# Top-32 attention into a capacity-dropping MoE: all products by the sign on GpSimd, the pick's table in PSUM, one order for all steps

## The chip, the cores and the metric

The kernel runs on one core of one Trainium2 chip. The metric is the device time of one execution in microseconds (us). The kernel before takes 996.0 us, the median of three runs (993.81, 996.0 and 996.81). The profiled execution took 994.79 us, with a span of 993.1 us from its first to its last instruction and a mean granted TensorE clock of 0.987.

## What is computed

The first part is attention over 8 batches and 8 heads, with 576 rows of 64 numbers per head. Of each row of scores only the 32 largest stay. The output, as 4608 tokens of 512 numbers, goes into a mixture of eight experts, each of which keeps at most 80 tokens.

```python
scores = scale * np.matmul(q, k.transpose(0, 1, 3, 2))          # (8, 8, 576, 576)
kth = np.partition(scores, -32, axis=-1)[..., -32:-31]
scores = np.where(scores >= kth, scores, -1e9)
attn = softmax(scores)                                          # exp, sum, divide
x = np.matmul(attn, v) -> (4608, 512)
expert_idx = argmax(x @ w_gate); gate_w = softmax(...)[expert_idx]
for e in range(8):
    tok = the (at most 80) tokens of expert e with the largest gate_w
    out[tok] = gate_w[tok] * (relu(x[tok] @ w1[e]) @ w2[e])
```

## The kernel before

**Tiling.** A pair of heads of one batch is one `n`; there are 32 of them. A *unit* is up to 128 score rows of one head, a tile of 128x576. A pair has nine units: four row blocks for each of the two heads (taken two by two, as `t` = 0 to 3 with `h` = 0 and 1), and one for the 64 rows left over of both heads together (`t` = 4, `h` = 2). That makes 288 units.

**What one unit goes through.** `front` (L216) multiplies the scores of one `t`, both heads at once, into four PSUM banks that `four` (L194) hands out, and ScalarE copies them to SBUF (L233, "the evacuation"). VectorE takes the eight largest of each of six groups of 96 (L241, letter G below), and then in three rounds the 24 largest of those 48 candidates (L252 and L260). With the 24th as a bar, ScalarE computes the sign of bar minus score, with its sum as a count (L257). The product of score and sign (L264, called `y`) turns what lies above the bar negative, so that a further maximum over 576 numbers (L266) finds the next eight. The *pick* (L269) compares the count with a table `past` of nine numbers and so chooses the threshold, the 32nd largest, out of nine candidates. `below` (L273) makes a mask from it: on GpSimd for even units (L280), on ScalarE for odd ones (L278). `turn_w` (L300) transposes scores and mask on TensorE, and ScalarE applies the exponential (L323 and L325). `back` (L328) multiplies by V, `over` (L340) takes the reciprocal of the sums on VectorE, and `divide` (L350) scales on ScalarE (L359).

**The order.** `run` (L428) writes the order out by hand (`manual_schedule`). A step `i` works on several units at once: G on unit `i`, the pieces b to e of the search on unit `i-1`, the product `y` on `i-2`, the maximum g on `i-3`, and the pick h and the mask m on `i-4`. A string of letters gives the order inside the step; odd and even steps have different strings (L459). The product is on GpSimd for odd units and on VectorE for even ones. After the letters a step emits, where they are due, `turn_w` of unit `i-4`, `divide`, `front` of unit `i+4`, and `back`. Every engine works through its own instructions in the order in which they are written, and waits by semaphores. So on ScalarE the work of a step is: the mask (odd units), the sign of unit `i-1`, the two exponentials, the two scalings, and last the evacuation of the scores of unit `i+4`. Of nine steps, five have a `front`. In three of the other four the same four banks serve another purpose: to transpose the next pair's Q and K (`turn`, copied at L214), to transpose the output (`norm`, copied at L376), and for the gate's logits (copied at L388).

**The scores' banks.** `four` takes a new tile from a pool of one buffer for each use. A use may begin when the readers of the use before are done.

**The weights.** The weights of experts 0 to 3 (4 MB for each) are loaded during the attention, in `slow`. Those of expert 4 are loaded when the attention's SBUF is free (`finish`, L733), and those of experts 5 to 7 when an earlier expert is done with its buffer.

Of the kernel before, what the change touches and what calls it, by code (L numbers as in the profile page):

```python
# [27 lines left out]
def kernel(  # L28
# [120 lines left out]
    class Attention:  # L149


        def __init__(self, stack, lean):
            self.lean = lean
            pool = lambda name, bufs, **kw: stack.enter_context(tc.tile_pool(name=name, bufs=bufs, **kw))
            self.nat, self.qkp, self.rows = pool("nat", 1), pool("qkp", 2), pool("rows", 2)
            self.small, vpool = pool("small", 4), pool("vpool", 1)
            self.ps_s, self.ps_w, self.ps_c = (pool(n, k, space=PSUM) for n, k in (("ps_s", 1), ("ps_w", 1), ("ps_c", 2)))
            self.qk, self.turned, self.lg = {}, {}, {}
            self.s, self.top, self.cnt, self.y, self.mask, self.w, self.xn = ({} for _ in range(7))
            self.thr, self.z = thr_all, z_all  # L160
            self.odd = set()


            self.vb = []
            for j in range(1 if lean else 3):
                t = vpool.tile([P, NK, 2, D + 1], F32, name=f"vb{j}")
                nc.gpsimd.memset(t[:, :, :, D : D + 1], 1.0)
                nc.gpsimd.memset(t[: P - TL, NF, :, :], 0.0)
                self.vb.append(t)

            self.xT = vpool.tile([P, NK * P], F32, name="xT")
            nc.gpsimd.memset(self.xT[:, S:], 0.0)
# [18 lines left out]
                t[P - TL :, NF, :, :D], v[one, 2 * hp : 2 * hp + 2, NF * P :, :].rearrange("o h p d -> p (o h) d"))  # L191
            self.qk[n] = tiles

        def four(self):  # L194
            return self.ps_s.tile([P, 4, 512], F32, name="sp", tag="sp")

        def turn_in(self, ps, t, cs=range(NK)):

# [3 lines left out]

        def turn(self, n):

            four = self.four()
            ps = [four[:, 2 * j : 2 * j + 2, :].rearrange("p j c -> p (j c)") for j in range(2)]
            both = self.qkp.tile([P, 2, S], F32, name="both", tag="both")
            self.turned[n] = both[:, 0, :], both[:, 1, :]
            for j, src in enumerate(self.qk.pop(n)):
                self.turn_in(ps[j], src.rearrange("p c h d -> p c (h d)"))  # L210
                if n == 0:
                    nc.scalar.copy(both[:, j, :], ps[j][:, :S])
            if n > 0:
                nc.scalar.copy(both, four.rearrange("p (k j) c -> p k (j c)", k=2)[:, :, :S])  # L214

        def front(self, n, t):  # L216

            qT, kT = self.turned[n]
            m = P if t < NF else TL
            i = n * UPP + 2 * t  # L220
            ps = self.four()
            for j in range(2):
                for h in range(2):
                    d = slice(D * h, D * h + D)
                    o = ps[:, 2 * h + j, :HS] if t < NF else ps[TL * h : TL * h + TL, j, :HS]
                    nc.tensor.matmul(o, lhsT=qT[d, t * P : t * P + m], rhs=kT[d, j * HS : (j + 1) * HS], start=True, stop=True)  # L226
            g = 2 if t < NF else 1
            s = self.rows.tile([P, 2 * S], F32, name="s", tag="s", bufs=2 if self.lean else 5)
            for h in range(g):
                self.s[i + h] = s[:, h * S : (h + 1) * S]  # L230
            for j in range(0, 2 * g, 2 if i == 0 else 2 * g):
                w = 2 if i == 0 else 2 * g
                nc.scalar.activation(s[:, j * HS : (j + w) * HS].rearrange("p (j c) -> p j c", c=HS), ps[:, j : j + w, :HS],  # L233
                                     Act.Copy, scale=TINY)

        def parts(self, i):
# [8 lines left out]
        def search(self, i):  # L245

            s, cand = self.s[i], self.top[i]
            top = self.top[i] = self.small.tile([P, G0 // 8 - 1, 8], F32, name="top", tag="top")
            w9 = self.small.tile([P, 16], F32, name="w9", tag="w9")
            for r in range(G0 // 8):  # L250
                dst = top[:, r, :] if r < G0 // 8 - 1 else w9[:, :8]
                nc.vector.max(out=dst, in_=cand)  # L252
                if r == G0 // 8 - 1:

                    sign = self.rows.tile([P, S], BF16, name="sign", tag="sign")
                    cnt = self.small.tile([P, 1], F32, name="cnt", tag="cnt")
                    nc.scalar.activation(sign, s, Act.Sign, bias=w9[:, 7:8], scale=-1.0, accum_out=cnt)  # L257
                yield
                if r < G0 // 8 - 1:
                    nc.vector.match_replace(out=cand, in_to_replace=dst, in_values=cand, imm_value=LOW)  # L260
                    yield
            y = self.rows.tile([P, S], F32, name="y", tag="y", bufs=1)
            engine = nc.gpsimd if i in self.odd else nc.vector
            engine.tensor_tensor(out=y, in0=s, in1=sign, op=Alu.mult)  # L264
            yield
            nc.vector.max(out=w9[:, 8:], in_=y)  # L266
            yield
            pick = self.small.tile([P, TOP_K - G0 + 1], F32, name="pick", tag="pick")
            nc.vector.scalar_tensor_tensor(out=pick, in0=past, scalar=cnt, in1=w9[:, 7:], accum_out=self.thr[:, i : i + 1],  # L269
                                           op0=Alu.is_equal, op1=Alu.mult)  # L270
            yield

# [9 lines left out]
        def search_all(self, i):  # L282

            s = self.s[i]
            top = self.top[i] = self.small.tile([P, TOP_K // 8, 8], F32, name="top", tag="top")
            scr = self.rows.tile([P, S], F32, name="y", tag="y", bufs=1)
            nc.vector.max(out=top[:, 0, :], in_=s)
            for r in range(1, TOP_K // 8):
                nc.vector.match_replace(out=scr, in_to_replace=top[:, r - 1, :], in_values=s if r == 1 else scr,
                                        imm_value=LOW)  # L290
                nc.vector.max(out=top[:, r, :], in_=scr)
            nc.vector.tensor_copy(self.thr[:, i : i + 1], top[:, TOP_K // 8 - 1, 7:8])
# [7 lines left out]
        def turn_w(self, n, t):  # L300
# [2 lines left out]
            g = 2 if t < NF else 1  # L303
            if i == NU - 1 and not self.lean:

                ab = self.four().rearrange("p h (c r) -> p h c r", r=P)
            else:
                ab = self.ps_w.tile([P, 2, NF, P], F32, name="ab", tag="ab")
            cc = self.ps_c.tile([P, 512], F32, name="cc", tag="cc")
# [51 lines left out]
        def norm(self, n, b, hp, bi, nb, cs=range(NK)):  # L361
# [7 lines left out]
            if NF in cs:  # L369
                nc.sync.dma_start(xv[one, NF * P :, cols].rearrange("o p d -> p o d"), xn[:TL, NF:, :])  # L370
            yield 1
            ps = self.four()[:, :2, :].rearrange("p j c -> p (j c)")
            at = slice(cs[0] * P, min(S, cs[-1] * P + P))
            self.turn_in(ps, xn, cs)
            xT = self.xT
            nc.scalar.copy(xT[:, at], ps[:, at])  # L376
            yield 1
            lp = self.four()[:, 0, : NK * E].rearrange("p (c e) -> p c e", e=E)
            for c in cs:
                for r in range(0, P, TL):  # L380
                    nc.tensor.matmul(lp[r : r + TL, c, :], lhsT=xT[:, c * P + r : c * P + r + TL], rhs=wg[:, hp, :],
# [46 lines left out]
        def run(self, slow):  # L428
# [17 lines left out]
            def step(i, last):  # L446
# [8 lines left out]
                    first[i] = self.parts(i)  # L455

                back = dict(a=0, b=1, c=1, d=1, e=1, y=2, g=3, h=4, m=4)

                for c in "ghmGbGycGdGGGeaz" if i % 2 else "GbGhmgcGdGeGGyaz":  # L459
                    if c == "G":  # L460
                        if 0 <= i < NU:
                            next(first[i])
                    elif c == "a":
                        if 0 <= i < NU:
                            next(first[i], None)
                            second[i] = self.search(i)
                            next(second[i])
                    elif c == "z":
                        for u in drawn:
                            self.over(*u)  # L470
                    elif c == "m":
                        if 0 <= i - back[c] < NU:
                            self.below(i - back[c])
                    elif i - back[c] in second:
                        next(second[i - back[c]])
# [257 lines left out]
    def finish(wpool, full):  # L733

        stack = ctx.enter_context(ExitStack())
        late = stack.enter_context(tc.tile_pool(name="late", bufs=1))
        for dma in load_w(4, late):
            dma()
        sl = stack.enter_context(tc.tile_pool(name="sl", bufs=1))
        fs = stack.enter_context(tc.tile_pool(name="fs", bufs=2))  # L740
        ps_x = stack.enter_context(tc.tile_pool(name="ps_x", bufs=2, space=PSUM))
# [119 lines left out]

    slow = clear()
    with ExitStack() as main:
        wpool = main.enter_context(tc.tile_pool(name="wpool", bufs=4))
        for e in range(4):
            slow += load_w(e, wpool, 4)
        with ExitStack() as stack:
            att = Attention(stack, False)
            att.run(slow)
        finish(wpool, False)  # L870
    with tc.If(nc.values_load(bad[0:1, 0:1]) > 0):
# [4 lines left out]
            with tc.For_i(0, B) as b:  # L876
                att.batch(b)
        with ExitStack() as again:
            wpool = again.enter_context(tc.tile_pool(name="wpool2", bufs=4))
            for e in range(4):  # L880
                for dma in load_w(e, wpool):
                    dma()
            finish(wpool, True)
# [31 lines left out]
```

## Time and profile before

| what | number |
|---|---|
| time, median of three | 996.0 us |
| span of the profiled execution | 993.1 us |
| attention: from the start to about 869 us; routing and experts after it | |
| VectorE busy | 870.6 us (88%) |
| TensorE busy / its weight loads | 885.5 us (89%) / 704.9 us (71%) |
| ScalarE busy | 797.2 us (80%) |
| GpSimd busy | 451.9 us (46%) |
| product `y` on VectorE / on GpSimd | 144 of 747 ns / 144 of 1283 ns |
| mask on GpSimd / on ScalarE | 144 of 1723 ns / 144 of 780 ns |
| pick on VectorE | 288 of 241 ns in the mean |
| evacuation of the scores on ScalarE | 161, 1040 ns in the mean |

The shares of busy time are means over the whole span, in which the attention takes seven eighths. An instruction's duration reaches from its start to its end; where an engine overlaps the start of one with the end of the one before, the distance from start to start is shorter, and the durations add up to more than the busy time.

### The profile page before, as it was taken

Reading aid. Unit: us, or ns where it says so; the run is one execution under the profiler, and the core shown is the slowest. Engines: PE = TensorE matmul, PEld = TensorE weight load, DVE = VectorE, ACT = ScalarE, POOL = GpSimd, SP = SyncE. Lnnn points to the kernel's source line nnn. Section 1 sums busy time; section 2 is a strip of 40 time slices with the busy share of each in tenths; the row PEclk is TensorE's granted clock in tenths of the full one; section 3 lists DMA queues with packets and bytes.
Section 4 is the critical chain, followed back from the end, with each engine's and each line's share of the span. In section 5 each row is a group of like instructions: output and inputs, shape, how many; then the busy total and the mean of one; then the engine's idle time right before and its main releaser. Section 6 shows DMA issues by size and latency. Waiting matters only on the chain.

```text
span 993.1 us, 35590 instructions
## 1 busy us (share of the span) xinstructions
PE 885.5 (89%) x13368; PEld 704.9 (71%) x13368; DVE 870.6 (88%) x5072; ACT 797.2 (80%) x1652; POOL 451.9 (46%) x330
## 2 busy tenths in 40 slices
PE   5899999998989989899899999999899898679996
PEld 3677777776767777677677777777677676668896
DVE  5899999999999999999999999999999999571110
ACT  3899999999999989999999999999899999601110
POOL 2445555555455545554555555555455555302111
PEclk9999999999999999999999999999999999979998
DMA  3344453333332323333333322222222100044920
GB/s 72 97 126 131 129 134 92 92 92 92 91 79 62 87 82 86 92 92 93 88 82 83 91 49 51 50 50 50 50 50 49 41 23 14 16 170 142 382 76 28
DMA packets 167893, 85.76 MB, mean 86 GB/s; under 512 B 117792, under 2 KB 154656, under 8 KB 167712
## 3 DMA queue, kind: packets, MB, share of 16 engines
q1 hardware_dynamic: 166688, 80.78, 29.7%
q0 software_dynamic: 1024, 2.62, 0.9%
q8 instruction: 107, 1.75, 0.7%
q14 instruction: 74, 0.61, 0.2%
HBM read 63.19 MB, written 20.19 MB: 84 GB/s over the span
## 4 chain that ended last, share of the span: by engine, by line
DVE 53%; PE 24%; ACT 18%; issue 5%; DMA 1%; POOL 0%; POOLq 0%; SPq 0%; ACTq 0%; DVEq 0%
DVE cand L241 17%; DVE w L266 12%; DVE cand L260 6%; DVE y L264 6%; ACT s L233 4%; DVE top L252 4%; PE yp L799 4%; ACT wT L325 3%; PE sp L201 3%; PE cc L336 3%; ACT sign L257 3%; DVE pick L269 3%; ACT mask L278 2%; PE sp L226 2%; PE ab L316 2%
## 5 line engine op out<-in xcount | busy, mean ns | idle before, releaser
L241 DVE MAX8 cand<-s 128x8 f32<-128x96 f32 x1728 | 393.9, 250 | 8.9 <-ACT s L233 8.8
L280 POOL TENSOR_SCALAR mask<-s,thr_all 128x576 bf16<-128x576 f32 x144 | 248.2, 1723 | 144.9 <-DVE pick L269 121.8
L264 POOL TENSOR_TENSOR y<-s,sign 128x576 f32<-128x576 f32 x144 | 184.8, 1283 | 277.3 <-DVE pick L269 128.0
L336 PEld LDWEIGHTS cc<-vb,wT 128*64 128x64 f32 x5760 | 181.7, 138 | 111.2 <-ACT wT L325 98.5
L257 ACT ACTIVATE sign<-s,w 128x576 bf16<-128x576 f32 x288 | 225.4, 783 | 22.8 <-DVE w L252 22.2
L336 PE MATMUL cc<-vb,wT 128*64 128x65 f32 x5760 | 204.0, 225 | 40.6 <-ACT wT L325 38.9
L266 DVE MAX8 w<-y 128x8 f32<-128x576 f32 x288 | 217.8, 756 | 2.5 <-POOL y L264 2.5
L226 PE MATMUL sp<-both 64*128 64x288 f32 (+1 forms) x1280 | 202.1, 435 | 15.0 <-ACT part L388 6.5
L233 ACT ACTIVATE s<-sp 128x1152 f32<-128x1152 f32 (+1 forms) x161 | 167.3, 1040 | 12.7 <-PE sp L226 11.9
L316 PE MATMUL ab<-ident,s 128*128 128x128 f32 x1148 | 175.6, 282 | 0.0
L325 ACT ACTIVATE wT<-ab 128x1024 f32<-128x1024 f32 (+1 forms) x159 | 148.8, 936 | 0.0
L226 PEld LDWEIGHTS sp<-both 64*128 64x128 f32 (+1 forms) x1280 | 105.6, 179 | 53.8 <-ACT part L388 8.5
L316 PEld LDWEIGHTS ab<-ident,s 128*128 128x128 f32 x1148 | 127.5, 141 | 11.6 <-issue 0.9
L321 PEld LDWEIGHTS <-mask 128*128 128x128 bf16 x1440 | 92.1, 98 | 42.4 <-ACT mask L278 19.6
L252 DVE MAX8 top<-cand 128x8 f32<-128x48 f32 x576 | 116.9, 203 | 0.0
L260 DVE MATCH_REPLACE8 cand<-top,cand 128x48 f32<-128x48 f32 x576 | 112.9, 196 | 0.0
L278 ACT ACTIVATE mask<-s,thr_all 128x576 bf16<-128x576 f32 x144 | 112.3, 780 | 0.4
L264 DVE TENSOR_TENSOR y<-s,sign 128x576 f32<-128x576 f32 x144 | 107.6, 747 | 4.5 <-ACT sign L257 4.5
L359 ACT ACTIVATE xn<-cc,z_all 128x64 f32<-128x64 f32 (+1 forms) x320 | 86.5, 318 | 1.4 <-DVE z_all L348 0.8
L316 PE MATMUL cc<-ident,s 128*128 128x128 f32 x288 | 78.9, 274 | 0.3 <-ACT xn L359 0.2
L269 DVE SCALAR_TENSOR_TENSOR pick<-past,cnt,w 128x9 f32<-128x9 f32 x288 | 69.5, 241 | 0.2 <-DVE z_all L348 0.2
L323 ACT ACTIVATE wT<-cc 128x256 f32<-128x256 f32 (+1 forms) x160 | 56.2, 351 | 12.0 <-PE cc L321 11.3
(188 smaller groups left out, 965.7 us busy)
## 6 DMA issues: line engine op xcount, KB each, us to landing
w<-in_moe_w_dram SPq DMA_DIRECT2D x32, 512.0 KB, 4.7
w<-in_moe_w_dram SPq DMA_DIRECT2D x8, 2048.0 KB, 9.8
out_dram<-zero SPq DMA_DIRECT2D x9, 1024.0 KB, 6.3
qn<-in_q_dram SPq DMA_DIRECT2D x64, 128.0 KB, 2.6
kn<-in_k_dram SPq DMA_DIRECT2D x64, 128.0 KB, 2.5
vb<-in_v_dram SPq DMA_DIRECT2D x64, 128.0 KB, 2.6
xd<-xn SPq DMA_DIRECT2D x32, 256.0 KB, 4.3
qn<-in_q_dram SPq DMA_DIRECT2D x32, 32.0 KB, 2.5
```

The source lines that it names most:

```text
L226: nc.tensor.matmul(o, lhsT=qT[d, t * P : t * P + m], rhs=kT[d, j * HS : (j + 1) * HS], start=True, stop=True)
L233: nc.scalar.activation(s[:, j * HS : (j + w) * HS].rearrange("p (j c) -> p j c", c=HS), ps[:, j : j + w, :HS], Act.Copy, scale=TINY)
L241: nc.vector.max(out=cand[:, j, :], in_=s[:, j * S // NG : (j + 1) * S // NG])
L252: nc.vector.max(out=dst, in_=cand)
L257: nc.scalar.activation(sign, s, Act.Sign, bias=w9[:, 7:8], scale=-1.0, accum_out=cnt)
L260: nc.vector.match_replace(out=cand, in_to_replace=dst, in_values=cand, imm_value=LOW)
L264: engine.tensor_tensor(out=y, in0=s, in1=sign, op=Alu.mult)
L266: nc.vector.max(out=w9[:, 8:], in_=y)
L280: nc.gpsimd.tensor_scalar(self.mask[i], self.s[i], self.thr[:, i : i + 1], None, op0=Alu.is_lt)
L316: nc.tensor.matmul(dst[h][c], lhsT=sc[:, keys[c]], rhs=ident, start=c == 0 or (c == NF and h == 0), stop=False, is_transpose=True, skip_gr ...
L325: nc.scalar.activation(wT[:, : g * NF, :], ab.rearrange("p h c r -> p (h c) r")[:, : g * NF, :], Act.Exp, scale=scale / TINY)
L336: nc.tensor.matmul(cc[r : r + TL, o], lhsT=wT[:, h * NF + c if c < NF else 2 * NF + h, r : r + TL], rhs=vb[:, c, h if t < NF else r // TL, ...
```

## The change

The change has four parts.

1. **All products on GpSimd.** The product `y` no longer alternates between the engines. Its buffer becomes two deep. This takes 144 instructions of a saturated VectorE away.
2. **One order for all steps.** With that, odd and even steps no longer differ, and one string serves both: the pick and the mask come first in the step, then the product, then the search, and the maximum g over the product comes late.
3. **The pick's table in PSUM.** The four banks become one tile, `banks`, that stays allocated. Each use of it gets a view by `four(w, step)`. The last 16 columns of the fourth bank, which no use of the banks writes, hold a copy of the table `past`, and the pick reads it there. The pick then has one large input in SBUF and not two.
4. **The weights of expert 3** are loaded late as well, like those of expert 4, which makes room in SBUF for the second buffer of `y`.

```diff
@@ Attention.__init__
-            self.ps_s, self.ps_w, self.ps_c = (pool(n, k, space=PSUM) for n, k in (("ps_s", 1), ("ps_w", 1), ("ps_c", 2)))
+            ps_s, self.ps_w, self.ps_c = (pool(n, k, space=PSUM) for n, k in (("ps_s", 1), ("ps_w", 1), ("ps_c", 2)))
+            self.banks = ps_s.tile([P, 4 * 512], F32, name="banks")
+
+            self.past = self.banks[:, 4 * 512 - 16 :][:, : TOP_K - G0 + 1]
+            nc.vector.tensor_copy(self.past, past)
@@
-        def four(self):
-            return self.ps_s.tile([P, 4, 512], F32, name="sp", tag="sp")
+        def four(self, w, step=512):
+
+            t = self.banks[:, :]
+            return bass.AP(t.tensor, t.offset, [list(t.ap[0]), [step, 4 * 512 // step], [1, w]])
@@ front (turn, turn_w and norm likewise take their views from four)
-            ps = self.four()
+            ps = self.four(HS)
@@ search
-            y = self.rows.tile([P, S], F32, name="y", tag="y", bufs=1)
-            engine = nc.gpsimd if i in self.odd else nc.vector
-            engine.tensor_tensor(out=y, in0=s, in1=sign, op=Alu.mult)
+            y = self.rows.tile([P, S], F32, name="y", tag="y")
+            nc.gpsimd.tensor_tensor(out=y, in0=s, in1=sign, op=Alu.mult)
...
-            nc.vector.scalar_tensor_tensor(out=pick, in0=past, scalar=cnt, in1=w9[:, 7:], accum_out=self.thr[:, i : i + 1],
+            nc.vector.scalar_tensor_tensor(out=pick, in0=self.past, scalar=cnt, in1=w9[:, 7:], accum_out=self.thr[:, i : i + 1],
                                            op0=Alu.is_equal, op1=Alu.mult)
@@ run
-                for c in "ghmGbGycGdGGGeaz" if i % 2 else "GbGhmgcGdGeGGyaz":
+                for c in "hmybGcGdGeGGGgza":
@@ finish
-        late = stack.enter_context(tc.tile_pool(name="late", bufs=1))
-        for dma in load_w(4, late):
-            dma()
+        late = stack.enter_context(tc.tile_pool(name="late", bufs=2))
+        for e in (3, 4):
+            for dma in load_w(e, late):
+                dma()
@@
-        wpool = main.enter_context(tc.tile_pool(name="wpool", bufs=4))
-        for e in range(4):
+        wpool = main.enter_context(tc.tile_pool(name="wpool", bufs=3))
+        for e in range(3):
             slow += load_w(e, wpool, 4)
```

More of the change, by code (lines that the diff above doesn't have):

```diff
@@ L203, in turn @@
         def turn(self, n):
-            four = self.four()
-            ps = [four[:, 2 * j : 2 * j + 2, :].rearrange("p j c -> p (j c)") for j in range(2)]
+            ps = self.four(S, 1024)
             both = self.qkp.tile([P, 2, S], F32, name="both", tag="both")
@@ L209, in turn @@
             for j, src in enumerate(self.qk.pop(n)):
-                self.turn_in(ps[j], src.rearrange("p c h d -> p c (h d)"))
+                self.turn_in(ps[:, j, :], src.rearrange("p c h d -> p c (h d)"))
                 if n == 0:
-                    nc.scalar.copy(both[:, j, :], ps[j][:, :S])
+                    nc.scalar.copy(both[:, j, :], ps[:, j, :])
             if n > 0:
-                nc.scalar.copy(both, four.rearrange("p (k j) c -> p k (j c)", k=2)[:, :, :S])
+                nc.scalar.copy(both, ps)
         def front(self, n, t):
@@ L224, in front @@
                     d = slice(D * h, D * h + D)
-                    o = ps[:, 2 * h + j, :HS] if t < NF else ps[TL * h : TL * h + TL, j, :HS]
+                    o = ps[:, 2 * h + j, :] if t < NF else ps[TL * h : TL * h + TL, j, :]
                     nc.tensor.matmul(o, lhsT=qT[d, t * P : t * P + m], rhs=kT[d, j * HS : (j + 1) * HS], start=True, stop=True)
@@ L232, in front @@
                 w = 2 if i == 0 else 2 * g
-                nc.scalar.activation(s[:, j * HS : (j + w) * HS].rearrange("p (j c) -> p j c", c=HS), ps[:, j : j + w, :HS],
+                nc.scalar.activation(s[:, j * HS : (j + w) * HS].rearrange("p (j c) -> p j c", c=HS), ps[:, j : j + w, :],
                                      Act.Copy, scale=TINY)
@@ L285, in search_all @@
             top = self.top[i] = self.small.tile([P, TOP_K // 8, 8], F32, name="top", tag="top")
-            scr = self.rows.tile([P, S], F32, name="y", tag="y", bufs=1)
+            scr = self.rows.tile([P, S], F32, name="y", tag="y")
             nc.vector.max(out=top[:, 0, :], in_=s)
@@ L304, in turn_w @@
             if i == NU - 1 and not self.lean:
-                ab = self.four().rearrange("p h (c r) -> p h c r", r=P)
+                ab = self.four(1024, 2048).rearrange("p o (h c r) -> p (o h) c r", h=2, r=P)
             else:
@@ L371, in norm @@
             yield 1
-            ps = self.four()[:, :2, :].rearrange("p j c -> p (j c)")
+            ps = self.four(1024, 2048)[:, 0, :]
             at = slice(cs[0] * P, min(S, cs[-1] * P + P))
@@ L377, in norm @@
             yield 1
-            lp = self.four()[:, 0, : NK * E].rearrange("p (c e) -> p c e", e=E)
+            lp = self.four(NK * E, 2048)[:, 0, :].rearrange("p (c e) -> p c e", e=E)
             for c in cs:
@@ L878 @@
         with ExitStack() as again:
-            wpool = again.enter_context(tc.tile_pool(name="wpool2", bufs=4))
-            for e in range(4):
+            wpool = again.enter_context(tc.tile_pool(name="wpool2", bufs=3))
+            for e in range(3):
                 for dma in load_w(e, wpool):
```

## Prediction, made before the changed kernel was run

> **What bounds the kernel now.** I read the page first, for the engine that the chain of waits follows, then the busy time by windows, for the slack of the others, then the instructions in order of time over two steps, for who waits for whom.
>
> The page's chain (shares by engine) and two of its groups:
>
> ```profile
> DVE 53%; PE 24%; ACT 18%; issue 5%; DMA 1%; POOL 0%; POOLq 0%; SPq 0%; ACTq 0%; DVEq 0%
> ...
> L264 POOL TENSOR_TENSOR y<-s,sign 128x576 f32<-128x576 f32 x144 | 184.8, 1283 | 277.3 <-DVE pick L269 128.0
> ...
> L264 DVE TENSOR_TENSOR y<-s,sign 128x576 f32<-128x576 f32 x144 | 107.6, 747 | 4.5 <-ACT sign L257 4.5
> ```
>
> Two windows, the middle of the attention and the start of the experts (columns: window, length, then busy PE, PEld, DVE, ACT, POOL, each with its count, TensorE clock, DMA share, GB/s):
>
> ```profile
> 400.00:500.00 100.00, 90.43 (x1311) 70.91 (x1306) 99.37 (x594) 92.68 (x192) 50.97 (x34) 1.00 0.33 87
> ...
> 870.00:880.00 10.00, 5.14 (x52) 3.85 (x53) 8.26 (x32) 0.27 (x1) 0.57 (x3) 0.50 0.96 350
> ```
>
> VectorE never rests in the attention (99%), so it sets the pace there. ScalarE is close behind (93%), GpSimd is half idle. The groups between 100 and 800 us count 240 maxima over `y`, one for each step, so a step takes 700 / 240 = 2.92 us.
>
> Two steps in order of time (start us, us, engine, line; in brackets the idle time before and who ended it):
>
> ```profile
> 503.06 0.21 DVE L252 MAX8 top<-cand 128x8 f32<-128x48 f32 x1
> ...
> 503.23 0.78 ACT L257 ACTIVATE sign<-s,w 128x576 bf16<-128x576 f32 x1 [0.57 <-DVE w L252]
> ...
> 503.75 0.21 DVE L269 SCALAR_TENSOR_TENSOR pick<-past,cnt,w 128x9 f32<-128x9 f32 x1
> ...
> 505.82 1.14 ACT L233 ACTIVATE s<-sp 128x1152 f32<-128x1152 f32 x1
> ...
> 507.05 0.21 DVE L269 SCALAR_TENSOR_TENSOR pick<-past,cnt,w 128x9 f32<-128x9 f32 x1
> ...
> 508.62 0.19 DVE L252 MAX8 w<-cand 128x8 f32<-128x48 f32 x1
> ...
> 508.90 0.78 ACT L257 ACTIVATE sign<-s,w 128x576 bf16<-128x576 f32 x1 [0.39 <-DVE w L252]
> ...
> 509.68 0.36 ACT L323 ACTIVATE wT<-cc 128x256 f32<-128x256 f32 x1
> ...
> 509.94 1.01 ACT L325 ACTIVATE wT<-ab 128x1024 f32<-128x1024 f32 x1
> ...
> 510.85 0.52 ACT L359 ACTIVATE xn<-cc,z_all 128x64 f32<-128x64 f32 x2
> 511.24 1.15 ACT L233 ACTIVATE s<-sp 128x1152 f32<-128x1152 f32 x1
> ```
>
> The reader is to see the lag between the two engines. At 503.06 VectorE ends a step. ScalarE's part of *that* step begins at 503.23 with the sign and ends with the evacuation, at 505.82 + 1.14 = 506.96. By then VectorE has long made the next step's pick (503.75). Today this lag costs nothing, because the pick reads nothing that ScalarE's later work touches.
>
> [...] the pick's median is 214 ns, but its longest 1286, and its 69.5 us are 8 us above 288 x 0.214. [...] in the attention the clock is 1.00.
>
> **Part by part.**
>
> *Products to GpSimd.* 144 instructions leave VectorE. One costs 747 ns from start to end, but the next instruction starts 0.65 us after it (505.60 to 506.25), so 0.65 / 2 = 0.33 us per step: 2.92 becomes 2.59. GpSimd then has 1.283 + 1.723 / 2 = 2.15 us per step, still under that; `y` is written a step and a half before the maximum g reads it, so no wait comes from it.
>
> *Pick without its second SBUF input.* At most the 8 us of blocking above. A PSUM operand could itself cost: [...] the reciprocals of before, which read PSUM, take only 154 ns. I take 0 [...].
>
> *Expert 3's weights.* 4 MB more, behind the 4 MB of expert 4, which move at 350 GB/s in the window above: 12 us more, ending near 893 us on the time scale of before. Expert 3's first product is at 938.67 us. Hidden; cost 0.
>
> *The table in the scores' banks: a new wait.* This is what decides. In the built program of the changed kernel, 249 of the 288 picks wait for a ScalarE instruction that reads `banks`: 156 for the evacuation of the scores, 31 for `both` (Q and K), 31 for `xT`, 31 for the logits. It is each time that of the step just before. The other 39 have no such wait. In before no pick waits for ScalarE at all. Also each `front` waits for the pick of its own step, which comes early and costs little.
>
> Queued behind the waiting pick is the whole search of VectorE, and in it the 24th largest (L252 into `w`) for which ScalarE's next sign waits. But the evacuation stands *behind* that sign in ScalarE's order. So the two engines no longer run side by side but close a loop in every step: pick, search, sign, exponentials, scalings, evacuation, next pick. Its length in a full step, from the rows above:
>
> - pick to sign start: 508.90 - 507.05 = 1.85 us, with six maxima L241 between. The new order has three there; each takes 0.16 us from start to start: 1.85 - 0.49 = 1.36
> - sign start to the end of the evacuation: 511.24 + 1.15 - 508.90 = 3.49
> - hand-over to VectorE: as from `w` to sign, 508.90 - 508.81 = 0.09
>
> Together 4.94 us. Where the mask is on GpSimd (half of these steps) the exponentials wait for it: pick to mask 0.39, mask 1.72, hand-over and mask products 0.4, against a sign that ends at 1.36 + 0.78: about 0.3 more. One in four scales 64-row tiles, 0.25 more. Mean: 4.94 + 0.15 + 0.06 = 5.15 us. Nine steps then are:
>
> - four full steps: 4 x 5.15 = 20.6
> - the step that fronts the rest of 64 rows (no exponentials; the scalings wait for the reciprocal behind g; evacuation 0.65): 3.7
> - `both`: 1.36 + 0.78 + 1.13 + 0.09 = 3.4
> - `xT`: 1.36 + 0.78 + 0.64 + 0.09 = 2.9
> - logits, behind two short exponentials, half with the GpSimd mask: 3.4
> - the step without a wait: VectorE's 2.6
>
> Sum 36.6, or 4.07 us per step, against 9 x 2.92 = 26.3. Over 32 pairs 32 x 10.3 = 330 us more; all gains of the other parts lie inside the 2.6 and 1.36 and are counted. 996 + 330 = 1326, say 1325 us.
>
> **The rivals.** *The wait is hidden, and it is faster:* if evacuations were done before the picks came, ScalarE would bound: 0.93 x 2.92 = 2.71, with its waits for Q and K (17 us of 240 steps) 2.78, and 996 - 288 x 0.14 = 956 us. For it: VectorE's 99% and the 108 us taken off. Against it: the lag of 3.2 us from 503.75 to 506.96, and the fixed order on ScalarE. *The short steps absorb their waits* at VectorE's 2.6: 20.6 + 5 x 2.6 = 33.6, so 996 + 32 x 7.3 = 1230 us. For it: those copies could start early; against it: each stands behind a sign. *TensorE's clock halves*, as its load falls from 90% to about 65% of a step: the score products (1.24 us) and mask products (0.4) take twice as long ahead of the evacuation, some 5.5 us in nine steps, up to 1500 us. [...]
>
> **The numbers.** Forecast 0.85; short steps absorb 0.07; half clock 0.04; faster 0.03; the rest, with no change, 0.01. The hand-overs, two in each step, may be 0.04 to 0.14: 29 us either way. With [...] a fourth of the clock's 175 upward, and half way to the absorbing case downward: 1265 to 1400. Slower 0.96.
>
> **What would show it.** Right: VectorE's busy share in the attention falls to about 65%, with the pick as the instruction that its idle time stands before, released by ScalarE's evacuation (L238 then), some 1.5 us per step in the mean; no product on VectorE; ScalarE idle before the sign; the chain passing between VectorE and ScalarE in turn; the experts' part as long as now. Wrong: VectorE above 90%, or its idle time in front of the maximum over `y`, released by GpSimd; or experts that wait for a weight transfer.

## The result, and the profile after

The changed kernel takes **1320.99 us**, the median of four runs (1312.62 to 1325.34), against 994.9 us for the kernel before beside it. The ratio is 1.3265, with a 95% interval of 1.3193 to 1.3337. Lines of the code are four or five higher now: the pick is L273, the evacuation L238, the sign L262, the maxima of the search L257, the product L268. The span of the profiled execution is 1320.9 us. Of the four executions of e7 below, one took 1643.98 us against 1258.61 to 1270.4 of the others; it is left out of the figure there, and what slowed it is not known.

The page after, first its busy times and the row of granted clock, then the shares of the chain, then three groups (busy us, mean ns of one, idle time of the engine before them and who ended it):

```profile
PE 999.2 (76%) x13368; PEld 777.0 (59%) x13368; DVE 803.6 (61%) x4929; ACT 841.2 (64%) x1652; POOL 623.8 (47%) x474
...
PEclk9889998879989998878888898988989998987999
...
ACT 35%; DVE 27%; PE 21%; POOL 10%; issue 5%; DMA 2%; SPq 0%; ACTq 0%; POOLq 0%; DVEq 0%
...
L262 ACT ACTIVATE sign<-s,w 128x576 bf16<-128x576 f32 x288 | 223.3, 775 | 257.4 <-DVE w L257 257.0
...
L268 POOL TENSOR_TENSOR y<-s,sign 128x576 f32<-128x576 f32 x288 | 362.0, 1278 | 14.3 <-ACT sign L262 14.3
L273 DVE SCALAR_TENSOR_TENSOR pick<-banks,cnt,w 128x9 f32<-128x9 f32 x288 | 65.6, 228 | 398.4 <-ACT s L238 331.3
```

The reader is to see that no engine is full. VectorE, 88% busy before, has 61%. Its idle time of 398 us stands in front of one instruction, the pick, which runs for only 228 ns, and ScalarE's evacuation ends 331 us of it. In turn ScalarE stands idle for 257 us in front of the sign, for which VectorE's 24th largest is the releaser. The two groups name each other: that is what a loop looks like on a page. The chain says the same, passing to both of them in similar shares (35% and 27%), where before 53% of it lay with VectorE. The rest runs through TensorE's products (21%) and through GpSimd (10%), whose mask is in the loop of every second unit.

Two windows, the middle of the attention and the ten microseconds behind it (columns as in the prediction):

```profile
400.00:500.00 100.00, 72.56 (x953) 55.15 (x949) 65.92 (x422) 71.14 (x140) 54.32 (x39) 0.95 0.22 58
...
1195.00:1205.00 10.00, 4.66 (x49) 3.53 (x50) 8.22 (x32) 0.29 (x2) 0.00 (x0) 0.50 0.62 221
```

And one full step in order of time:

```profile
705.54 0.23 DVE L273 SCALAR_TENSOR_TENSOR pick<-banks,cnt,w 128x9 f32<-128x9 f32 x1 [0.27 <-ACT xT L380]
...
706.65 0.19 DVE L257 MAX8 w<-cand 128x8 f32<-128x48 f32 x1
706.94 0.78 ACT L262 ACTIVATE sign<-s,w 128x576 bf16<-128x576 f32 x1 [0.35 <-DVE w L257]
...
707.97 1.01 ACT L329 ACTIVATE wT<-ab 128x1024 f32<-128x1024 f32 x1
708.88 0.52 ACT L363 ACTIVATE xn<-cc,z_all 128x64 f32<-128x64 f32 x2
709.27 1.15 ACT L238 ACTIVATE s<-banks 128x1152 f32<-128x1152 f32 x1
710.45 0.23 DVE L273 SCALAR_TENSOR_TENSOR pick<-banks,cnt,w 128x9 f32<-128x9 f32 x1 [2.29 <-ACT s L238]
```

The order is the one of the prediction: pick, search up to `w`, sign, exponentials, scalings, evacuation, and only then the next pick, for which VectorE has been idle for 2.29 us. From pick to pick are 4.91 us, where before 3.30 lay between the two picks shown. The last copy of the attention's logits starts at 1194.85 us instead of 869.27, which is 325.6 us of the difference; what follows it takes 126.1 instead of 123.8.

### The profile page after: what moved, and what is told of

It reads as the page before. It is cut to its first block, busy times and chain, and to the rows that moved or that the text cites. A ratio compares the mean times of both kernels' runs of the same rounds, so it can differ in the third digit from the quotient of the medians.

```text
span 1320.9 us, 35608 instructions
## 1 busy us (share of the span) xinstructions
PE 999.2 (76%) x13368; PEld 777.0 (59%) x13368; DVE 803.6 (61%) x4929; ACT 841.2 (64%) x1652; POOL 623.8 (47%) x474
## 4 chain that ended last, share of the span: by engine, by line
ACT 35%; DVE 27%; PE 21%; POOL 10%; issue 5%; DMA 2%; SPq 0%; ACTq 0%; POOLq 0%; DVEq 0%
ACT s L238 11%; POOL mask L284 9%; DVE cand L246 9%; ACT sign L262 7%; ACT wT L329 5%; DVE cand L265 5%; PE banks L231 5%; DVE pick L273 5%; ACT xn L363 4%; DVE w L270 3%; PE yp L803 3%; PE cc L340 3%; ACT wT L327 3%; ACT both L219 2%; DVE top L257 2%
## 5 line engine op out<-in xcount | busy, mean ns | idle before, releaser
L262 ACT ACTIVATE sign<-s,w 128x576 bf16<-128x576 f32 x288 | 223.3, 775 | 257.4 <-DVE w L257 257.0
L246 DVE MAX8 cand<-s 128x8 f32<-128x96 f32 x1728 | 376.5, 246 | 8.4 <-ACT s L238 8.4
L268 POOL TENSOR_TENSOR y<-s,sign 128x576 f32<-128x576 f32 x288 | 362.0, 1278 | 14.3 <-ACT sign L262 14.3
L273 DVE SCALAR_TENSOR_TENSOR pick<-banks,cnt,w 128x9 f32<-128x9 f32 x288 | 65.6, 228 | 398.4 <-ACT s L238 331.3
L340 PEld LDWEIGHTS cc<-vb,wT 128*64 128x64 f32 x5760 | 221.3, 162 | 125.2 <-ACT wT L329 96.9
L340 PE MATMUL cc<-vb,wT 128*64 128x65 f32 x5760 | 245.3, 250 | 42.8 <-ACT wT L329 42.8
L231 PE MATMUL banks<-both 64*128 64x288 f32 (+1 forms) x1280 | 232.7, 489 | 27.8 <-DVE pick L273 23.3
L320 PE MATMUL ab<-ident,s 128*128 128x128 f32 x1148 | 188.2, 294 | 0.0
L238 ACT ACTIVATE s<-banks 128x1152 f32<-128x1152 f32 (+1 forms) x161 | 167.0, 1038 | 18.6 <-PE banks L231 17.7
L231 PEld LDWEIGHTS banks<-both 64*128 64x128 f32 (+1 forms) x1280 | 117.2, 198 | 73.5 <-DVE pick L273 24.8
L325 PE MATMUL cc<-minus,mask 128*128 128x128 bf16 x144 | 33.3, 231 | 151.4 <-POOL mask L284 151.4
L320 PEld LDWEIGHTS ab<-ident,s 128*128 128x128 f32 x1148 | 135.9, 148 | 12.5 <-issue 0.9
L257 DVE MAX8 top<-cand 128x8 f32<-128x48 f32 x576 | 111.0, 193 | 0.1
L320 PE MATMUL cc<-ident,s 128*128 128x128 f32 x288 | 82.7, 287 | 6.2 <-ACT xn L363 6.2
L325 PE MATMUL cc<-huge,mask 128*128 128x128 bf16 x144 | 33.4, 232 | 60.1 <-ACT mask L282 58.3
```

The costliest lines, as they stand in the source:

```text
L246: nc.vector.max(out=cand[:, j, :], in_=s[:, j * S // NG : (j + 1) * S // NG])
L268: nc.gpsimd.tensor_tensor(out=y, in0=s, in1=sign, op=Alu.mult)
L320: nc.tensor.matmul(dst[h][c], lhsT=sc[:, keys[c]], rhs=ident, start=c == 0 or (c == NF and h == 0), stop=False, is_transpose=True, skip_gr ...
L325: nc.tensor.matmul(dst[h][c], lhsT=mk[:, keys[c]], rhs=huge if i + h in self.odd else minus, start=False, stop=True, skip_group_check=True)
L340: nc.tensor.matmul(cc[r : r + TL, o], lhsT=wT[:, h * NF + c if c < NF else 2 * NF + h, r : r + TL], rhs=vb[:, c, h if t < NF else r // TL, ...
```

## The experiments

Theory: the table shares a bank with the scores, so that the pick waits for ScalarE, and ScalarE's order closes the wait to a loop. Rivals: the cost is that of the new order of the letters, of the product on the slower GpSimd, or of reading PSUM at all. In the diffs, lines with - are of the changed kernel, or of the kernel before where that is said.

**One word: the table back in SBUF (e2).**

```diff
-            nc.vector.scalar_tensor_tensor(out=pick, in0=self.past, ...
+            nc.vector.scalar_tensor_tensor(out=pick, in0=past, ...
```

> The changed kernel, whose pick reads the table in SBUF as before; one word of the source differs. No wait for the banks, but two SBUF inputs again, beside a GpSimd that is busy 2.15 us of each step. My theory: the loop opens as with a bank of its own, [...] 950 to 1060 us. Rival (order or late products): above 1250 us.

Measured: 1009.61 us, ratio 1.0133 (1.0113 to 1.0153). 311 of the 326 us are gone with that word, so the order, the product and the weights together, gains and the table's blocking included, cost at most 15 on balance. The pick's group between 100 and 800 us, and one of them beside GpSimd:

```profile
L273 DVE SCALAR_TENSOR_TENSOR pick<-past,cnt,w 128x9 f32<-128x9 f32 x236 | 129.2, 547 | 0.0
```

```profile
499.86 2.52 POOL L268 TENSOR_TENSOR y<-s,sign 128x576 f32<-128x576 f32 x2
500.29 0.87 DVE L273 SCALAR_TENSOR_TENSOR pick<-past,cnt,w 128x9 f32<-128x9 f32 x1
```

No idle time is left in front of it, but with both inputs in SBUF it now takes 547 ns in the mean, up to 1287, against 239 in the same window before. The second fence shows why: it ends 1.30 us after the start of the first of two products on GpSimd (499.86 to 501.16), which take 1.26 us each. It is so throughout: all 135 of the 288 picks that take over 300 ns end within 0.03 us of the end of a GpSimd instruction. The trace of before has the same blocking in few places: 17 of its 288 picks take 459 to 1286 ns, the others at most 232, and each of the 17 starts while a product on GpSimd runs and ends within 0.03 us of its end. Now the product is on GpSimd in every step. The pick that reads the table in PSUM is not held up: in the changed kernel 83 of the 288 overlap a product on GpSimd, and none takes over 231 ns. The blocking costs 0.547 - 0.239 = 0.31 us per step, nearly all of the 0.33 that the departure of the product gives VectorE. A step takes 700 / 236 = 2.97 us, against 2.92 before.

**The kernel before, with only the table moved (e3).** The tile `banks`, the views from `four` and the table in the last columns, with the old order and the products on both engines (- is the kernel before):

```diff
-            nc.vector.scalar_tensor_tensor(out=pick, in0=past, ...
+            self.past = self.banks[:, 4 * 512 - 16 :][:, : TOP_K - G0 + 1]
+            nc.vector.scalar_tensor_tensor(out=pick, in0=self.past, ...
```

> The kernel before with the table moved into the scores' banks and nothing else: products still on both engines, the two old orders, old weights. My theory: the same loop, and longer, since the old orders put one to three more maxima, and the product, between the pick and the next sign or the pick: about 4.5 us per step, 1380 to 1480 us. Rival (the loss comes from the new order or from GpSimd): within some per cent of the 996 us of before, at most 1050.

Measured: 1411.96 us, ratio 1.4161 (1.4122 to 1.42). A wait of the trace between 100 and 1100 us (us in total, times, longest):

```profile
DVE pick L273 <- ACT s L237: 278.5, 127, 3.2
```

The table in the scores' banks is enough for the loss, and dearer in the old order, where in odd steps six maxima stand between pick and sign and not three, and in even steps two and the maximum over `y`. The rivals fall: with the same order and the same product the time moves by 311 us when the table goes (e2), and without either by 415 when it comes.

**The scalings behind the evacuation (e7).** This shortens the loop by the two scalings and leaves the rest:

```diff
-                for u in done:
-                    self.divide(*u)
                 ...
                 if not rest:
                     back()
+                for u in done:
+                    self.divide(*u)
```

> The changed kernel with the two scalings (divide) emitted behind front, so that the evacuation comes 0.39 us sooner in ScalarE's order (0.64 where 64-row tiles are scaled). My theory, by the terms of the loop: in full steps with the mask on ScalarE 0.39 us less, with the mask on GpSimd only 0.17, because there the score products on TensorE end just then; in the step of the 64-row rest 0.75 less, which no longer waits for the reciprocal. Together 2.05 us of 9 steps, 66 us in all: 1255 us, 1235 to 1275. If the loop does not run through the evacuation: 1321 us.

Measured: 1270 us, ratio 1.2704 (1.2653 to 1.2755), which is 5.6% of the time before, some 56 us, under the change as it is. What stands ahead of the evacuation on ScalarE is on the path. A part of the 56 us may be TensorE's, whose mean clock is 0.931 here and 0.904 in the changed kernel.

**The scores before the transposes (e4).** `front` is emitted ahead of `turn_w`, to put the evacuation ahead of the exponentials:

```diff
+                if busy:
+                    self.front(*units[f][:2])
                 ...
                 if whole(i - 4):
                     self.turn_w(*units[i - 4][:2])
                 ...
-                if busy:
-                    self.front(*units[f][:2])
```

> The changed kernel with the front of a step emitted ahead of turn_w, so that on ScalarE the evacuation comes right behind the sign, ahead of the two exponentials and the scalings. The table stays beside the scores. My theory: the loop of a full step loses the exponentials and scalings, 1.56 us (pick to pick 3.4 instead of 4.9), part of which comes back in the step after, where ScalarE is still behind: about 3.2 us per step, 1040 to 1130 us. If the loop ran through something else (the mask on GpSimd, or TensorE at half its clock), it would stay at 1320 us within 2%.

Measured: 1412.06 us, ratio 1.4167 (1.4084 to 1.425): a miss, by some 300 us and in its sign. Waits between 100 and 1100 us:

```profile
DVE pick L273 <- ACT s L238: 199.2, 123, 3.6
...
ACT s L238 <- PE cc L320: 130.1, 99, 2.8
...
DVE pick L273 <- ACT both L219: 87.0, 25, 4.3
```

The evacuation doesn't come early: it waits in turn for TensorE's transposes (L320), since the buffer of `s` that it writes is one that these still read. I had looked at the order alone and not at the buffer. And where the product by V waits for the exponentials, the transposes of Q and K stand behind it, so that the copy into `both` comes later still.

**The table in a bank of its own (e1).** In `kernel.py` the attention's PSUM tiles come to eight banks of 512 columns: four for the scores, two for `ab`, two for `cc`. To stay at eight, one of them is freed. Scores of full rows go into three banks of 384 columns; the middle one takes the end of one head and the start of the other, with a copy of K in block-diagonal form, `kd`:

```diff
+            self.past = pool("ps_p", 1, space=PSUM).tile([P, 512], F32, name="table")[:, : TOP_K - G0 + 1]
...
+            nc.gpsimd.tensor_copy(kd[0:D, 0:192], both[0:D, 1, 384:S])
+            nc.gpsimd.tensor_copy(kd[D:P, 192:384], both[D:P, 1, 0:192])
...
+                for j, d, rhs in ((0, slice(0, D), kT[0:D, 0:384]), (2, slice(D, P), kT[D:P, 192:S]), (1, slice(0, P), kd)):
+                    nc.tensor.matmul(ps[:, j, :], lhsT=qT[d, t * P : t * P + m], rhs=rhs, start=True, stop=True)
```

> The changed kernel with the table still in PSUM, but in a bank that nothing else uses. The scores take three banks of 384 columns instead of four of 288; the middle one, which holds keys of both heads, is one product over all 128 rows with a block-diagonal K that two small GpSimd copies build for each pair of heads. Everything else (products on GpSimd, one order, late weights) stays. No pick waits for an evacuation. My theory (the loop is closed by the table's place in the scores' banks alone): the loop opens, VectorE needs 2.59 us per step, ScalarE about 2.8 with its own waits, so 940 to 985 us. Rival (the new order, or products that GpSimd delivers late, stall the search): it stays above 1250 us.

Measured: 1046.84 us, ratio 1.0518 (1.0486 to 1.0551). The loop is open, but a new wait of VectorE is there (100 to 700 us), and it lies above the forecast:

```profile
DVE w L279 <- POOL y L277: 73.4, 45, 3.9
```

The copies into `kd` stand in GpSimd's queue and wait for Q and K, and the products stand behind them. So two variants were built that fill `kd` in a later step, one with the table in its own bank (e5), one, otherwise equal, with the table in the last 16 columns of the third scores' bank (e6):

> The version with the table in a bank of its own, with two repairs: the two GpSimd copies for the block-diagonal K are emitted two steps later, so that GpSimd doesn't wait for ScalarE's copy of K and delay the product behind it (there VectorE waited 104 us for products), and the product over all 128 rows comes ahead of the two over 64 rows. My theory: the waits for products fall below 25 us; VectorE needs 2.6 us per step, ScalarE 2.8; 950 to 1000 us. Rival (TensorE, 93% busy in the first version, is its real bound): 1015 to 1045 us.

> The same kernel as the run before it in this call, except for one line: the table lies in the last 16 columns of the third bank of the scores, and not in a bank of its own. The instructions, their order and their operands' kinds are the same. My theory (the shared bank alone makes the loop): 1290 to 1350 us, with VectorE idle some 1.4 us per step in front of the pick. Rival: within 3% of the run with its own bank.

Measured: 3414.92 and 3785.0 us, whole times that say nothing here: for the first pairs `kd` was filled one step after its first use, and the program then repeats the attention on its second path. Read from 100 to 700 us alone, a step takes 600 / 206 = 2.91 us in e5 and 600 / 144 = 4.17 in e6. These two runs gave the forecasts for the pair that fills `kd` in time:

```diff
+                if fresh and fresh[0][0] == i:
+                    self.middle(fresh.pop(0)[1])        # the two copies into kd
```

and, the only difference of the second from the first:

```diff
-            self.past = pool("ps_p", 1, space=PSUM).tile([P, 512], F32, name="table")[:, : TOP_K - G0 + 1]
+            self.past = self.banks[:, 3 * 512 - 16 :][:, : TOP_K - G0 + 1]
```

> The changed kernel with the pick's table in a PSUM bank of its own and the scores in three banks (full rows multiply a block-diagonal copy of K for the middle bank); the block-diagonal copy is filled by two GpSimd copies as soon as K is transposed, not when the first front is due. Theory (the loop is only the shared bank; with the bank to itself TensorE bounds): no pick waits for ScalarE, a step takes about 2.91 us as on the main path of the variant that filled it too late, 980 to 1005 us in all. Rival (the late products and the wider score products still cost as when the copy was filled at the front): 1015 to 1045 us, with maxima of VectorE that wait for GpSimd's product.

> The same kernel as own_bank_c but for one line: the table lies in the last 16 columns of the third scores' bank and not in a bank of its own. Theory (the shared bank alone closes the loop): the pick waits for the evacuation again, about 4.17 us per step against 2.91, 1340 to 1370 us. Rival (what cost the time in the changed kernel is the order, or the product on GpSimd, or reading PSUM at all): within 3% of the kernel with a bank of its own.

Measured: **988.86 us** with a bank of its own, ratio 0.9936 (0.9914 to 0.9959), and 1363.92 us with the shared bank, ratio 1.367 (1.3595 to 1.3745). The pick's groups between 100 and 700 us, of the first and of the second kernel:

```profile
L287 DVE SCALAR_TENSOR_TENSOR pick<-table,cnt,w 128x9 f32<-128x9 f32 x206 | 44.9, 218 | 0.0
```

```profile
L287 DVE SCALAR_TENSOR_TENSOR pick<-banks,cnt,w 128x9 f32<-128x9 f32 x143 | 32.5, 227 | 219.6 <-ACT s L253 192.4 <-ACT both L222 11.6 <-ACT part L406 9.9
```

One line of code, 375 us. Both picks read PSUM and take about the same time, but only one has idle time before it. A read of PSUM is not what costs; the place that it reads is: a bank, and with it a tile of the program, that ScalarE reads too. Which of the two, bank or tile, makes the wait is not separated by this pair. And the kernel with the bank of its own is the one version here that beats the kernel before, by 7 us, or 0.4 to 0.9%. Its window in the middle of the attention:

```profile
400.00:500.00 100.00, 94.79 (x1276) 69.04 (x1274) 93.19 (x570) 92.63 (x192) 73.94 (x59) 1.00 0.29 75
```

TensorE leads with 95%, VectorE has 93 and ScalarE 93. By these shares the work taken from VectorE opens a gain only as far as the next engine; no run tests that.

**The weights alone (e8).** Part 4 in the kernel before (- is the kernel before):

```diff
-        late = stack.enter_context(tc.tile_pool(name="late", bufs=1))
-        for dma in load_w(4, late):
-            dma()
+        late = stack.enter_context(tc.tile_pool(name="late", bufs=2))
+        for e in (3, 4):
+            for dma in load_w(e, late):
+                dma()
```

> The kernel before with nothing but the weights of expert 3 loaded late, like those of expert 4. My theory: hidden; 0 to 2 us more than before (996 to 999 us). Rival: the experts wait for weights, 10 us or more.

Measured: 998.63 us, ratio 1.0041 (1.0024 to 1.0059), so 4 us more, between 2 and 6. Not quite nothing.

**TensorE's idle time filled (e11).** The clock row of the page after holds sevens and eights; half the clock was in force in 198 of the 1000 us between 100 and 1100. To price it, the kernel with the shared bank of e10 gets products of constants into a bank that is free there, at two places where TensorE waits:

```diff
+        def fill(self, k):
+            for _ in range(k):
+                nc.tensor.matmul(self.spare[:, :P], lhsT=huge, rhs=minus, start=True, stop=True, skip_group_check=True)
...
             for h in range(g):
+                if h == 1:
+                    self.fill(12)
...
                 if not rest:
+                    if whole(i - 5):
+                        self.fill(5)
                     back()
```

> The kernel of shared_bank_c (table in the last columns of the third scores' bank, 1363.92 us, granted clock 0.89 to 0.96 between 300 and 700 us) with idle TensorE time filled: in each pair of units 12 small bf16 products of constants into a spare PSUM bank while the mask of the second unit is waited for, and 5 more ahead of the products by V (some 1.0 us per pair, worked out from 0.06 us for each of the mask products from start to start). Nobody reads them. Theory (the clock is halved because TensorE rests a quarter of the time in many short waits): the granted clock rises to 0.97 or more, the waits in front of the pick stay, and the time falls by 15 to 40 us to 1325 to 1350. Rival (the halved clock has another cause, or costs nothing): the clock stays at 0.90 to 0.94 and the time is 1355 to 1385.

Measured: 1332.2 us, ratio 1.3377 (1.3342 to 1.3413), so with more work 32 us less than e10. The same window, of e10 and then of e11 (TensorE's busy time is the second number, the clock the third from the end):

```profile
400.00:500.00 100.00, 76.02 (x920) 51.86 (x919) 61.63 (x397) 68.28 (x136) 51.29 (x42) 0.93 0.24 63
```

```profile
400.00:500.00 100.00, 85.17 (x1130) 62.85 (x1132) 65.24 (x416) 71.40 (x140) 53.35 (x42) 1.00 0.27 67
```

TensorE is busy for 85 us of 100 and not 76, and the clock is 1.00 and not 0.93; over the span its mean rises from 0.921 to 0.965. Windows of 1 us show how it falls: in stretches of 3.4 us, or of twice that, at half speed. Between 300 and 700 us there are 19 such stretches in the changed kernel (82 us of half clock in all), 17 in e10 (61 us), 6 in e11 (20 us) and none in before. So TensorE's rests do slow the clock, and at this load that costs some 32 us, less only what the filling itself costs or saves elsewhere.

## Why the prediction was right, and where its steps were not

**The wait and the loop: right.** The picks wait for the ScalarE instruction of the step before, the chain goes between the two engines, and no product is on VectorE. The main term stands on four legs: the table moved alone costs as much and more (e3), taken back it frees nearly all (e2), moved to a bank of its own it frees all (e9 against e10), and the loop shortens with what stands in it (e7). No kernel was run in which the two engines touch the bank without a wait between them, so what the chip would do then is not shown here. Nor does every wait go back to a bank that both engines touch. The table lies in the fourth bank, and by `kernel.py` the copies of `xT` and of the logits and the evacuation of the 64-row rest read the first two banks alone. Yet the picks behind them wait: 7.2, 23.2 and 28.6 us between 100 and 1100 us, 59 of 343 in all. So the program orders accesses to the tile `banks` more widely than bank by bank. What a tile for each bank would have saved was not run.

**The size of the loop: right in its rows; the fit to 4 us is in part luck.** From pick to pick in the trace, 100 to 1100 us:

| step | forecast us | mean / median us |
|---|---|---|
| full, mask on ScalarE | 4.94 | 5.01 / 4.91 |
| full, mask on GpSimd | 5.24 | 5.43 / 5.22 |
| rest of 64 rows | 3.7 | 3.64 / 3.64 |
| `both` | 3.4 | 3.42 / 3.30 |
| `xT` | 2.9 | 2.88 / 2.83 |
| logits | 3.4 | 3.41 / 3.52 |
| no wait | 2.6 | 2.52 / 2.48 |
| all | 4.07 | 4.08 |

The five short steps come to 15.9 us by their means, where 16.0 were forecast. The full steps lie above their medians, and the clock, which was not in the sum, goes with that: 45 of the 109 full steps hold over 0.3 us of half clock and take 5.43 us in the mean, the other 64 take 5.07, where 5.15 were forecast. So a sum a little too long for full clock met a clock that was left out, and that 1325 is only 4 us from 1321 is luck to that extent.

**The rival of the half clock: mis-sized, and set aside for a reason that failed.** It got a chance of 0.04, since I took TensorE's rests to be too short for it; that was an estimate of mine, and no run shows how long a rest has to be. TensorE waits for GpSimd's mask, as the waits between 100 and 1100 us show, for up to 3.5 us:

```profile
PE cc L325 <- POOL mask L284: 129.7, 77, 3.5
```

I had followed only the loop through ScalarE, and not asked how long TensorE rests between the transposes of two units and the second unit's mask, where that comes from GpSimd and no score product lies between. Nor do the falls keep to such long waits: of the gaps between 300 and 700 us, by TensorE's records, only five are longer than 3 us, against 19 stretches of half clock. The trace of before says the same: the half clock of its window at 870 us begins at 868.35, and TensorE's longest gap between 850 and 900 us is 2.86.

What goes with the fall is the busy share of a whole window. All stretches of half clock in the changed kernel begin and end on one grid of 3.41 us. One fall, with the window ahead of it and the one behind (columns as in the prediction):

```profile
309.39:312.80 3.41, 1.55 (x13) 0.97 (x13) 2.36 (x14) 2.15 (x5) 3.33 (x3) 1.00 0.43 98
312.80:316.21 3.41, 3.41 (x47) 3.23 (x46) 1.93 (x15) 2.75 (x6) 0.87 (x1) 0.50 0.00 0
316.21:319.62 3.41, 2.85 (x52) 2.00 (x52) 2.55 (x17) 1.88 (x6) 1.59 (x1) 1.00 0.02 5
```

Of the windows of that grid between 100 and 1100 us, 48 at full clock are followed by half clock, and TensorE is busy for 7 to 62% of them, 43 in the median. The 187 that are followed by full clock have 49% or more, 77 in the median. Why those between 49 and 62% go either way stays open.

The cost was far under the 175 us that I gave this rival, since the clock is halved for a part of the time only: about 32 us by e11 and e10, where the mean clock is 0.921; taken over to the changed kernel, with 0.904, that is an estimate.

**The stall in front of the pick: right.** 1.5 us per step were forecast. Between 100 and 1100 us 245 picks have 342.7 us of idle time before them, 1.40 each. VectorE's share of 65% is met as well (66 in the window above).

**The other parts.** The product on GpSimd: VectorE waits 1.2 us for it over the whole changed kernel, so no wait to speak of, as said. The pick's operand in PSUM at 0: right, with a median of 228 ns against 214. The blocking at "at most the 8 us": right for the kernel before and wrong as a price of part 3, because part 1 changes it. With every product on GpSimd the blocking is 0.31 us per step (e2), some 89 us over 288 steps, ten times as much. Without part 3, part 1 is worth nothing here; the two belong together. That did not touch the number, in which both parts are made and lie inside the loop. The weights at 0: mis-sized by 4 us (e8).

**The rival that was faster: refuted for this kernel, and too hopeful in itself.** With the wait taken away it was to be 956 us, with ScalarE as the bound. The kernel without the wait (e9) takes 988.86, with TensorE ahead of the others. That kernel multiplies a wider middle bank (1.72 us from the first to the last score product of a full step, 502.73 to 504.45 in the trace of its neighbour e10, against the 1.24 of before), so 956 is not shown to be out of reach; a kernel with a bank for the table and the old score products was not built. "Short steps absorb their waits" is refuted by the table: those with a wait take 2.9 to 3.6 us, not 2.6.

## What to carry to other kernels

Here a constant parked in a spare corner of a busy PSUM tile inherited the waits of that tile, or of its banks, for 375 us (e10 against e9): look for who else touches them between two reads, and where that engine's own work depends on the reader, count the length of the loop and not the length of the read. To price a new wait, follow both engines' orders through one step; the sum of the rows from the reader to the release was good to 0.03 us in the full steps here, by their medians. When work moves to GpSimd, price again each small VectorE instruction with two inputs in SBUF, since it can give back nearly all that the move gains (0.31 of 0.33 us per step in e2).

## What had not been expected of the hardware

- TensorE, 75% busy, ran at half its clock for a fifth of the time, in stretches of 3.4 us or twice that. They follow windows of 3.41 us that it was busy for 7 to 62% of, mostly without a rest of over 3 us. Full clock came back behind windows at half clock that it was busy for 90% or more of (48), and stayed away behind those with 59 to 91% (10). Busy for 83 to 85%, it had a clock of 0.95 to 1.00 in four windows of 100 us (e11).
- Work that nobody reads made a kernel 2.3% faster (1363.92 to 1332.2 us).
- The blocking beside GpSimd reaches other small instructions. The addition of the gate's logits (L392 before, L396 after; mostly 128x40, two inputs in SBUF) has a median of 182 ns before and 820 after; 16 of the 25 take over 500 ns there, and each of them overlaps a product on GpSimd and ends within 0.06 us of its end.
